# Splitting the second block of a seven-product matrix step, and giving the last tile the common order

## The chip, the cores and the metric

The kernel runs on one NeuronCore of a Trainium2 chip. The metric is the device time of one execution in microseconds (us). Before the change the median of three runs is 280.29 us (279.97 to 280.5). TensorE (PE) multiplies matrices and adds into PSUM banks, VectorE (DVE) and ScalarE (ACT) work element by element and empty PSUM, GpSimd (POOL) prepares some inputs and issues loads, SyncE (SP) issues the stores. Each engine runs its own instructions in order and waits for the others by semaphores.

## The reference

Two parts follow each other. The first is attention over pooled keys and values: for each of 8 batches and 8 heads, 576 queries of 64 elements meet 72 keys, each the mean of 8 neighbours.

```
scores = scale * q @ k_pooled.T          # 576 x 72 for each batch and head
attn   = exp(scores - max) ; attn /= sum(attn) + 1e-9
x      = attn @ v_pooled                  # 4608 tokens x 512 after joining the heads
h      = x @ w_in                         # 512 x 2048
g      = h * sigmoid(h)
out    = g @ w_out                        # 2048 x 512, float32
```

## The kernel before

The 4608 tokens are worked in nine tiles of 512, t = 0 to 8. Tile 0 uses plain products. Tiles 1 to 8 use `tile_products`, where both products of the second part are done as 2 x 2 block products with seven block multiplications in place of eight, plus additions of blocks. While tile t is multiplied, the attention of batch t + 1 is woven in between, so tiles 1 to 6 carry attention work and tiles 7 and 8 (called bare) carry none.

The order of the work in a tile is a written list of items. The first product is cut in four units a, b, c, d, and `a1` is block multiplication 1 of unit a, with four matmuls. `as`, `bs`, `cs`, `ds` only apply the activation to a finished block. For the second product, `P2` is the first half of block multiplication 2 and `Q2` its second half; `o2:4-5` is the part of it from contraction block 4 up to 5. Each of the eight contraction blocks of a multiplication is one **step** of two matmuls of 128x256 (L608, one for each half c of the tokens), so `P2` and `Q2` have four steps each. A step of a unit also has two matmuls. Tiles 2 to 6 follow `FOUR`, which ends in `HEAD`; tile 1 follows `THREE`, a text of its own; tiles 7 and 8 follow `BARE`, in which the second product is written out and `HEAD` isn't used. For tile 8 some text replacements are applied (L861). In a tile of `FOUR` the steps of the first product are 0 to 53 (and 62, 63 for `d4`); `P1` and `Q1` are 54 to 61, and the second product goes on from 64 to 111.

The second product uses three PSUM banks. Bank A takes multiplication 1, is copied to bank B by DVE (L618, in `behind`), and then takes multiplication 2 on top. Bank E takes multiplication 5; ACT copies it into SBUF as p (L621). B takes multiplication 6; then DVE forms E = B + p (L623). Then multiplication 7 goes on top of B, 3 on top of E, 4 on top of B. So the first step of `P7` writes the bank that L623 has just read, and must wait for it. When multiplication 2 ends, `second(2)` makes DVE copy A to the output tile (L653); the stores are issued after multiplication 3 (both 256-column halves together) and 4. In tile 8, B is split in two banks, one for each c, and L660 stands for L623, once for each half.

Multiplications 5, 6, 7, 3 take as their left operand sums of hidden blocks, `h_sum[0]` to `h_sum[3]`, formed by DVE (L537) in halves of four contraction blocks for sums 0, 1 and 2. `h_sum[0]` and `h_sum[1]` need the activations of `d4` and `ds`.

The banks come from two rings, `mm` of three and `at` of five. In tiles 2 to 6, a tile takes seven banks from `mm`, in this order: bank B of units a, b, c, d, then A, B, E of the second product. The attention takes its banks from `at`.

The attention, the sums and the loads are **fillers**: each has a step number s and is emitted just before step s + 1, wherever the list of items then is. In tiles 2 to 6 the sums stand at 64 to 66, at 77 the first denominators (den_ps L348, then ACT's lnd L357 and rec L358) and the second scores (sc_ps L330, then four exponentials es L338), at 87 the second denominators and two sets of numerators (nu_ps L374, then DVE's xT L383), and at 94 the third scores. Fillers keep their step number when the items are reordered.

Of the kernel before, what the change touches and what calls it, by code (L numbers as in the profile page):

```python
# [36 lines left out]
def kernel(  # L37
# [759 lines left out]
    def load_half_2(name, half):  # L797
        for i0, i1 in ((0, SA), (SA, SLOTS), (SLOTS, SLOTS + 1)):
            load_slots(nc.gpsimd, 2, name, i0, i1, half)

    HEAD = "P1 ds Q1 d4 P2 Q2 P5 Q5 P6 Q6 P7 Q7 P3 Q3 P4 Q4"
    FOUR = (
        "a1 a5 b1 b5 a6 a2 b6 b2 a7 a3 b7 b3 as a4 c1 c5 bs b4 d1 c6 c2 d5 d6 c7 c3 d2 d7"
        " cs d3 c4 " + HEAD
    )
# [9 lines left out]
    for t in range(NT):  # L815
# [42 lines left out]

        order = ORDER.get(t, FOUR if a < B else BARE)
        if t == NT - 1:  # L860
            order = order.replace("P4 Q4", "R4 S4").replace("o5:0-1 o2:0-3 o5:1-8", "o5:0-2 o2:0-2 o5:2-8").replace("o2:3", "o2:2")  # L861
        o = 2 if t == 1 else 0
        f = []

# [95 lines left out]
```

## Time and profile before

| what | value |
|---|---|
| time, median of three runs | 280.29 us |
| the profiled execution's own time | 280.23 us |
| its span, first to last instruction | 278.4 us |
| TensorE busy | 270.7 us (97%) |
| VectorE busy | 209.6 us (75%) |
| ScalarE busy | 190.6 us (68%) |
| GpSimd busy | 97.3 us (35%) |
| DMA, mean over the span | 135 GB/s |
| granted TensorE clock | full in all 40 slices |

In the profile PE is a matmul, PEld the load of its stationary operand, L608 a line of the kernel and o_psA, o_psB, o_psE the three banks of the second product. A line of the timeline gives the start, the length, the engine, the line and operation, what is written from what, and how many instructions are merged. Times count from the start of the span. The second product of tile 2 starts at 93.15 us, those of tiles 3 to 6 at 121.85, 150.55, 179.19 and 207.84, of tile 7 at 236.49 and of tile 8 at 261.08.

### The profile page before, as it was taken

What the parts mean: (1) busy time and instruction counts of PE and PEld (TensorE: products, weight loads), DVE (VectorE), ACT (ScalarE), POOL (GpSimd) and SP (SyncE); (2) the same over time, 40 slices, a digit from 0 to 9 for tenths busy, and PEclk for the clock granted to TensorE, in tenths of its full rate; (3) what the DMA queues carried; (4) which work ended last, traced back from release to release, by engine and by line L of the source; (5) the groups of instructions that cost most, each with busy time, mean ns of one, the idle gap of its engine ahead of it and who ended that gap; (6) DMA issues with size and microseconds to landing.
All of it is one profiled execution on the core that took longest, in us unless ns stands there. A gap on an engine that the chain in (4) does not pass through costs nothing.

```text
span 278.4 us, 7274 instructions
## 1 busy us (share of the span) xinstructions
PE 270.7 (97%) x2952; PEld 212.4 (76%) x2959; DVE 209.6 (75%) x388; ACT 190.6 (68%) x376; POOL 97.3 (35%) x102
## 2 busy tenths in 40 slices
PE   8999999999999999999999999999999999999994
PEld 4448544488788878887888778877887788888883
DVE  4787886987997867876787687777787686766872
ACT  1677766568669785979497958885798678409700
POOL 8665217232138520962087219850900000000000
PEclk9999999999999999999999999999999999999999
DMA  7999999897747896569556966998410032004004
GB/s 213 279 254 244 207 325 190 219 160 140 150 55 153 222 169 116 130 164 172 96 118 167 168 103 156 189 110 130 122 31 0 4 77 76 2 19 115 20 2 151
DMA packets 31473, 37.72 MB, mean 135 GB/s; under 512 B 10352, under 2 KB 22384, under 8 KB 31440
## 3 DMA queue, kind: packets, MB, share of 16 engines
q0 software_dynamic: 23792, 26.64, 52.4%
q1 hardware_dynamic: 7216, 9.97, 12.8%
q10 hardware_dynamic: 432, 0.66, 0.7%
q8 instruction: 23, 0.38, 0.6%
q14 instruction: 10, 0.08, 0.1%
HBM read 36.70 MB, written 9.44 MB: 166 GB/s over the span
## 4 chain that ended last, share of the span: by engine, by line
PE 87%; ACT 6%; DVE 4%; issue 1%; DVEq 0%
PE u_psB L589 14%; PE o_psB L608 13%; PE o_psA L608 10%; PE u_psA L589 10%; PE u_psE L589 10%; PE o_psE L608 9%; PE hp_ps L474 6%; PE o_ps L509 3%; PE sc_ps L330 3%; ACT es L338 3%; PE warm_ps L708 2%; PE den_ps L348 2%; DVE o_psE L623 2%; PE nu_ps L374 1%; DVE xT L383 1%; ACT rec L358 1%
## 5 line engine op out<-in xcount | busy, mean ns | idle before, releaser
L608 PEld LDWEIGHTS <-h_sum 128*128 128x128 bf16 x512 | 48.7, 98 | 10.1 <-issue 2.2
L589 PEld LDWEIGHTS <-w_sum 128*128 128x128 bf16 x496 | 48.2, 98 | 5.7
L338 ACT ACTIVATE es<-sc_ps 72x384 bf16<-72x384 f32 (+1 forms) x100 | 39.0, 469 | 13.9 <-PE sc_ps L330 13.8
L608 PEld LDWEIGHTS <-h_T 128*128 128x128 bf16 x384 | 36.5, 98 | 6.1 <-issue 1.1
L589 PEld LDWEIGHTS <-w_in_sb 128*128 128x128 bf16 x372 | 36.3, 98 | 4.4
L589 PE MATMUL u_psA<-xT,w_in_sb 128*128 128x256 bf16 x248 | 37.4, 273 | 0.0
L589 PE MATMUL u_psB<-x_sum,w_sum 128*128 128x256 bf16 x248 | 36.7, 273 | 0.0
L608 PE MATMUL o_psB<-w_sum,h_sum 128*128 128x256 bf16 x256 | 31.8, 273 | 1.4 <-DVE o_psE L623 1.4
L608 PE MATMUL o_psA<-w_out_sb,h_T 128*128 128x256 bf16 x256 | 31.0, 272 | 0.0
L618 DVE COPY u_psB<-u_psA 128x512 f32<-128x512 f32 x31 | 21.4, 697 | 10.5 <-PE u_psA L589 10.3
L623 DVE TENSOR_TENSOR u_psE<-u_psB,p 128x512 f32<-128x512 f32 x31 | 20.9, 693 | 9.7 <-ACT p L621 8.6
L627 ACT ACTIVATE h_T<-u_psE 128x512 bf16<-128x512 f32 x31 | 18.5, 597 | 11.2 <-PE u_psE L589 11.0
L383 DVE TENSOR_TENSOR xT<-nu_ps,rec 128x384 bf16<-128x384 f32 (+1 forms) x50 | 23.8, 530 | 0.2
L183 POOL TENSOR_TENSOR raw<-raw 72x1024 f32<-72x1024 f32 x10 | 23.6, 2362 | 0.0
L640 DVE TENSOR_TENSOR c<-u_psB,p 128x512 f32<-128x512 f32 x31 | 21.0, 680 | 3.1 <-PE u_psB L589 2.3
L537 DVE TENSOR_TENSOR h_sum<-h_T 128x1024 bf16<-128x1024 bf16 (+1 forms) x31 | 21.3, 698 | 1.1 <-ACT h_T L627 1.1
L627 ACT ACTIVATE h_T<-u_psB 128x512 bf16<-128x512 f32 x31 | 18.6, 600 | 4.4 <-PE u_psB L589 4.4
L537 DVE TENSOR_TENSOR h_sum<-h_T,h_sum 128x1024 bf16<-128x1024 bf16 (+1 forms) x24 | 20.4, 858 | 0.1
L627 ACT ACTIVATE h_T<-c 128x512 bf16<-128x512 f32 x31 | 19.7, 637 | 0.0
L627 ACT ACTIVATE h_T<-u_psA 128x512 bf16<-128x512 f32 x31 | 18.8, 607 | 1.2 <-PE u_psA L589 1.0
L357 ACT ACTIVATE lnd<-den_ps 128x384 f32<-128x384 f32 (+1 forms) x23 | 11.1, 484 | 11.9 <-PE den_ps L348 11.7
L474 PE MATMUL hp_ps<-xT,w_in_sb 128*128 128x288 bf16 (+2 forms) x122 | 18.8, 303 | 0.2
(87 smaller groups left out, 466.6 us busy)
## 6 DMA issues: line engine op xcount, KB each, us to landing
out_dram<-o_sb SPq DMA_DIRECT2D x128, 64.0 KB, 1.7
raw<-in_k_dram POOLq DMA_DIRECT2D x10, 576.0 KB, 8.6
raw<-in_v_dram POOLq DMA_DIRECT2D x10, 576.0 KB, 8.1
q_bf<-in_q_dram POOLq DMA_DIRECT2D x6, 576.0 KB, 9.1
w_in_sb<-in_moe_w_in_dram POOLq DMA_DIRECT2D x8, 256.0 KB, 8.4
w_out_sb<-in_moe_w_out_dram POOLq DMA_DIRECT2D x4, 512.0 KB, 13.3
raw<-in_v_dram POOLq DMA_DIRECT2D x2, 768.0 KB, 11.1
raw<-in_k_dram POOLq DMA_DIRECT2D x1, 768.0 KB, 9.5
```

Of the source, the lines that this page charges most:

```text
L183: nc.gpsimd.tensor_add(out=raw[:, :, : 2 * D], in0=raw[:, :, : 2 * D], in1=raw[:, :, 2 * D :])
L338: nc.scalar.activation(es[:, s, :], sc[s], func=AF.Exp, scale=score_scale)
L357: nc.scalar.activation(lnd, den_ps[:, :w], func=AF.Ln)
L383: nc.vector.tensor_mul(out=xT[:, 2 * g0 + c : 2 * (g0 + ng - 1) + c + 1 : 2, cols], in0=nu[c][:, :w].rearrange("r (g n) -> r g n", g=ng), ...
L474: nc.tensor.matmul(hp_ps[:, r0:r1], lhsT=w_in_sb[:, kk, g * 128 : (g + 1) * 128], rhs=xT[:, kk, x0 : x0 + r1 - r0], start=(kk == 0), stop= ...
L537: nc.vector.tensor_tensor(out=h_sum[n][:, k0:k1, :], in0=get(a), in1=get(b), op=op)
L589: nc.tensor.matmul(ps[y, BANK[n]][:, u, :], lhsT=w[:, kk, 128 * u : 128 * (u + 1)], rhs=x[:, kk, :], start=n in (1, 5) and u == 0 and kk == 0,
L608: nc.tensor.matmul(o_bank(n, c), lhsT=left(n, kt, c), rhs=w[:, kt, :], start=n in (1, 5) and kt == 0 and c == 0, stop=kt == KQ - 1, skip_g ...
L618: vcopy(out=ps[y, "B"], in_=ps[y, "A"])
L623: tt(out=ps[y, "E"], in0=ps[y, "B"], in1=f32[y], op=add)
L627: nc.scalar.activation(h_T[:, g : g + 2, j * NQ : (j + 1) * NQ], src, func=AF.Silu)
L640: tt(out=c22, in0=ps[y, "B"], in1=f32[y], op=add)
```

## The change

In tiles 2 to 6, multiplication 2 is cut after its fifth step. Its last three steps, and with them DVE's copy of bank A, now come after multiplication 6 and ahead of 7; multiplications 5 and 6 come three steps earlier. In tile 8 the two replacements that gave it an order of its own are gone, so that it has the order of tile 7 (save its last two items): one step of 5, three of 2, seven of 5, then 6, and the other five of 2. Tile 8 had two, two, six, and then the other six of 2. Nothing is added or left out; the number of matmuls, copies, sums and stores is the same.

```diff
-    HEAD = "P1 ds Q1 d4 P2 Q2 P5 Q5 P6 Q6 P7 Q7 P3 Q3 P4 Q4"
+    HEAD = "P1 ds Q1 d4 P2 o2:4-5 P5 Q5 P6 Q6 o2:5-8 P7 Q7 P3 Q3 P4 Q4"
...
         if t == NT - 1:
-            order = order.replace("P4 Q4", "R4 S4").replace("o5:0-1 o2:0-3 o5:1-8", "o5:0-2 o2:0-2 o5:2-8").replace("o2:3", "o2:2")
+            order = order.replace("P4 Q4", "R4 S4")
```

## The prediction

> **What bounds the kernel now.** I read the page first (busy shares, the chain that ended last), then the waits of PE, then the timeline of one tile of 2 to 6 and of the last tile, engine by engine.
>
> ```profile
> PE 270.7 (97%) x2952; PEld 212.4 (76%) x2959; DVE 209.6 (75%) x388; ACT 190.6 (68%) x376; POOL 97.3 (35%) x102
> ...
> PE 87%; ACT 6%; DVE 4%; issue 1%; DVEq 0%
> ```
>
> PE is the bound, and the chain leaves it for ACT and DVE in only a tenth of the span. So the change is worth what it takes from PE's holes. The waits of PE name two that it touches:
>
> ```profile
> PE o_psB L608 <- DVE o_psE L623: 1.4, 6, 0.3
> ...
> PE o_psE L608 <- DVE h_sum L537: 0.2, 1, 0.2
> ```
>
> The first stands six times, once in each of tiles 1 to 6, ahead of P7. The second is in the last tile. In tile 2 PE runs:
>
> ```profile
> 95.92 1.91 PE L608 MATMUL o_psA<-w_out_sb,h_T 128*128 128x256 bf16 x16
> 97.66 1.47 PE L608 MATMUL o_psE<-w_sum,h_sum 128*128 128x256 bf16 x12
> 99.07 0.37 PE L348 MATMUL den_ps<-es,ones 72*32 72x384 bf16 x4
> 99.37 0.54 PE L330 MATMUL sc_ps<-qT,kz 32*72 32x192 bf16 x16
> 99.84 0.61 PE L608 MATMUL o_psE<-w_sum,h_sum 128*128 128x256 bf16 x4
> 100.28 1.91 PE L608 MATMUL o_psB<-w_sum,h_sum 128*128 128x256 bf16 x16
> 102.12 0.34 PE L348 MATMUL den_ps<-es,ones 72*32 72x384 bf16 x4
> 102.30 0.83 PE L374 MATMUL nu_ps<-es,vp 72*32 72x192 bf16 x32
> 103.36 1.69 PE L608 MATMUL o_psB<-w_sum,h_sum 128*128 128x256 bf16 x14 [0.23 <-DVE o_psE L623]
> ```
>
> Sixteen matmuls take 97.66 - 95.92 = 1.74 us, so one takes 0.109 and a step 0.218. P7 could have started at 103.06, when its first weight load runs (in the same place P4 starts 0.43 after the start of 16 numerator matmuls; 16 more take 0.33, and 102.30 + 0.76 = 103.06). It started at 103.36, when L623 was through: 0.30 lost. ACT and DVE show why L623 was late:
>
> ```profile
> 99.54 0.49 ACT L357 ACTIVATE lnd<-den_ps 128x384 f32<-128x384 f32 x1 [0.48 <-PE den_ps L348]
> 100.06 0.52 ACT L358 ACTIVATE rec<-lnd 128x384 f32<-128x384 f32 x1
> 100.50 1.60 ACT L338 ACTIVATE es<-sc_ps 72x384 bf16<-72x384 f32 x4
> 101.98 0.59 ACT L621 COPY p<-o_psE 128x512 f32<-128x512 f32 x1
> ```
>
> ```profile
> 96.98 0.68 DVE L537 TENSOR_TENSOR h_sum<-h_T 128x1024 bf16<-128x1024 bf16 x1
> 97.58 0.68 DVE L537 TENSOR_TENSOR h_sum<-h_T,h_sum 128x1024 bf16<-128x1024 bf16 x1
> ...
> 102.60 0.70 DVE L623 TENSOR_TENSOR o_psE<-o_psB,p 128x512 f32<-128x512 f32 x1 [2.25 <-ACT p L621]
> 103.21 1.94 DVE L383 TENSOR_TENSOR xT<-nu_ps,rec 128x384 bf16<-128x384 f32 x4
> ```
>
> The copy p stands on ACT behind lnd, rec and four exponentials, because the fillers at step 77 come inside Q5. L623 then waits 2.25 us for p, and PE for L623. In the last tile the late one is the second half of h_sum[0]:
>
> ```profile
> 263.70 0.60 PE L608 MATMUL o_psE<-w_sum,h_sum 128*128 128x256 bf16 x4
> 264.14 0.60 PE L608 MATMUL o_psA<-w_out_sb,h_T 128*128 128x256 bf16 x4
> 264.58 0.60 PE L608 MATMUL o_psE<-w_sum,h_sum 128*128 128x256 bf16 x4
> 265.33 1.05 PE L608 MATMUL o_psE<-w_sum,h_sum 128*128 128x256 bf16 x8 [0.16 <-DVE h_sum L537]
> ```
>
> **Part 1, tiles 2 to 6.** Moved: six matmuls and their weight loads, and DVE's copy L653. No DMA moves: the store of that output tile is issued after Q3, far behind. The number of steps is the same, so the fillers stay where they are in time; den_ps and the scores now fall after the first step of P6 instead of inside Q5.
>
> *The wait at P7.* P5 starts at 95.92 + 5 x 0.218 = 97.01, P6 at 98.75. In tiles 7 and 8 p starts 0.25 after P6's first matmul (241.63 to 241.88; 266.22 to 266.47), so here at 99.00, ahead of lnd, and is done at 99.6 instead of 102.57. Multiplication 6 ends three steps ahead of 102.02, at 101.37; by tile 8's lag (Q6's end at 267.96, DVE's start at 268.12) to tile 7's (243.37, 243.64), L623 runs from about 101.6 to 102.3. P7 at 103.06 finds it done. Cover left: 0.7 us. Gain 0.30, and by the same reading 0.30, 0.29, 0.30 and 0.30 in tiles 3 to 6 (P7 at 132.06, 160.75, 189.40, 218.04 against 131.76, 160.46, 189.10, 217.74): 1.49 in all.
>
> The idle figures beside P7 are 0.22 or 0.23, 1.12 in sum for the five; I take starts against starts, since those are recorded. The Trainium skill, Perfetto Trace Analysis, section on the Tensor Engine instruction, says that a matmul's reported end is an estimate from its size and no observation. By the idle rows alone the whole change would come to 279.0 rather than 278.6.
>
> *p goes ahead of lnd, rec, es on ACT.* Behind it wait den_ps of step 87, and through it PE. ACT is idle 0.48 before lnd. Where nothing else holds the next instruction, ACT starts it 0.46 to 0.48 after p (256.64 to 257.10; 232.04 to 232.51), so lnd could start at 99.48, ahead of its 99.54: no cost. With the 0.62 of the p at 101.98 (there lnd waited for den_ps) it is 99.62: 0.08 later. The far end is p's whole 0.59, if it starts only when the idle time is over. The exponentials end at 102.10, and den_ps needs the last for its fourth matmul, so a delay reaches PE nearly in full. I take 0.01 a tile, 0.05 in all, near the unit rows since they show the same copy followed at once; ends 0 and 5 x 0.59 = 2.9.
>
> *P5 and Q5 come 0.65 earlier.* Their operands: the first half of h_sum[0] starts at 95.78 and is done at 96.46, needed at 97.01. The second half (the 96.98 row) is done at 97.66, needed at 97.88; after 0.06 from DVE's end to PE's start (265.27 to 265.33) 0.16 us is left. h_sum[1]'s second half, done at 98.26, is needed at about 99.8 to 100.4. Bank E's ring slot was unit d's, read by ACT from 95.53 to 96.13: 0.88 of slack. All zero; the thin one is Q5, 0.16. The other tiles have the same distances within 0.02.
>
> *L653 on DVE.* It goes behind L623, ends at about 102.95, and ahead of four xT. These now start at 102.9 instead of 103.21, if nu_ps is there (last numerators' start 102.9). Behind them PE's scores at step 94 wait for the third xT's bank: 102.9 + 3 x 0.485 = 104.35, needed at 104.67. Zero; were L653 0.3 later, its excess would count.
>
> *Bank A is held longer*, till 102.95 in place of 99.23. Its ring slot goes next to unit a of the next tile, filled by DVE's copy at 110.94: 8 us of slack, cost nothing. The Trainium skill, PSUM — Partial Sum Buffer, summary of rules, advises to evacuate promptly, which speaks against the change; it gives no price. If the 3.7 us of longer holding were a wait each time, the sum would be 18 us worse; the row's 8 us of slack say nothing of the kind happens.
>
> **Part 2, tile 8.** P5 to P6 is 263.70 to 266.22, 2.52 us for 20 matmuls that need 2.18: 0.34 lost. Tile 7 has the new order, and there it is 239.11 to 241.63, also 2.52, with 22 matmuls: 0.12 lost. So P6 stays put and one step more of multiplication 2 fits into the hole; five are left behind Q6 instead of six. P7 could start at 267.96 + 10 x 0.109 = 269.05 instead of 269.27. Its second matmul, at 269.16, needs L660's second half, which ends at 269.09, plus 0.06: 269.15. Just done. Its other edge: multiplication 2 starts at 263.92 in place of 264.14, and needs A's copies (L651, 263.03 to 263.80, plus 0.06): 0.06 left. Gain 0.22 at most, 0 at the lower end if both edges bind; I take 0.17.
>
> **Sum.** 1.49 - 0.05 + 0.17 = 1.6 from the profiled execution's 280.23: 278.6. That execution stands 0.06 below the median 280.29, so 278.7. Everything behind these points (xT, x_sum, POOL's gate, the next tile's first steps) is released by PE or follows it, with DVE and ACT idle before L670 and L672, so it moves along.
>
> **The rivals.**
>
> *Part of the gain goes into den_ps.* p delays lnd by 0.1 to 0.25, and PE waits at step 87 rather than at P7. For: only 0.06 of room on ACT. Against: the copies in the units. Five times 0.1 to 0.25 off: 279.2 to 279.9.
>
> *No gain.* Another release holds P7 at 103.36, or the scores at step 94 take the wait (bank release by xT). For: the step sits among attention fillers that wait on one another. Against: P7 has no wait other than L623's in the waits of PE. Then only tile 8 gains: 280.0 to 280.4.
>
> *Slower: Q5 waits for h_sum.* P5 and Q5 have come closer to sums that DVE makes in one run from 95.78 to 98.26. If the first step waits for the whole of h_sum[0], P5 stands from 97.01 to 97.72, 0.71 a tile; less the 0.30 gained, 0.41 x 5 - 0.17 = 1.9 worse: 282.1. Against: in tile 8 two steps of 5 run at 263.70, ahead of the second half's start at 264.58, so halves are tracked apart. It decides once the sums come 0.46 later than now (0.16 of room plus the 0.30 gained); one more DVE operation of 0.60 ahead of them would do.
>
> **How the numbers follow.** The forecast with its own range of 278.2 to 279.2 has 0.70; the partial gain 0.13; no gain 0.07; slower 0.10. A difference under 0.2%, 0.56 us, can't be told from none, so faster means below 279.73: 0.70 + 0.12 = 0.82; within, 0.01 + 0.07 = 0.08; slower 0.10. The range 278.2 (all of 1.49 + 0.34, and 0.3 for the spread of runs shown) to 279.9 holds the first two cases and leaves out 0.17 and a little of the first.
>
> **What would show it.** Right: the wait of P7 on L623 falls from six to one (tile 1), p starts right after P6's first matmuls, L623's wait for p is gone, P6 to P7 in tile 2 has no hole. Wrong: a wait of den_ps on es, of o_psE on h_sum, or of sc_ps on xT in each of tiles 2 to 6; or in tile 8, o_psB waiting on L660. The likeliest mistake is the 0.06 on ACT and the 0.16 at Q5, both taken from rows that end that close.

## The result, and the profile after

The median of six runs is 278.38 us (278.04 to 279.0) against 280.28 us of six runs of the kernel before (279.73 to 280.54). The ratio is 0.9935, 95% interval 0.992 to 0.9951, or 1.4 to 2.2 us. The forecast was 278.7, faster. One execution in a second timing of the changed kernel (below) took 456.98 us at a granted clock of 0.56, and is left out of that timing's median.

The page of the changed kernel, the busy shares and the chain that ended last:

```profile
PE 270.6 (98%) x2959; PEld 211.3 (77%) x2959; DVE 209.7 (76%) x388; ACT 190.7 (69%) x376; POOL 97.3 (35%) x102
...
PE 93%; DVE 4%; DMA 2%; issue 0%; DVEq 0%
```

ACT had 6% of the chain before and is no longer among the shares listed. The busy times of PE, DVE, ACT and POOL are within 0.1 us of those before; PE's 270.6 us now lie in a span of 276.3 us. The waits of PE, as the profile lists them:

```profile
PE warm_ps L708 <- DVE warm L727: 1.2, 1, 1.2
PE o_psB L608 <- DVE o_psE L623: 0.3, 1, 0.3
PE kz_ps L275 <- DVE k L257: 0.2, 1, 0.2
```

The wait of P7 on L623 is left once, in tile 1, whose order isn't changed; that of the last tile on h_sum is gone from the list. The timeline of tile 2 after the change, PE from P2 to P7:

```profile
95.33 1.25 PE L608 MATMUL o_psA<-w_out_sb,h_T 128*128 128x256 bf16 x10
96.41 1.91 PE L608 MATMUL o_psE<-w_sum,h_sum 128*128 128x256 bf16 x16
98.16 0.38 PE L608 MATMUL o_psB<-w_sum,h_sum 128*128 128x256 bf16 x2
98.47 0.37 PE L348 MATMUL den_ps<-es,ones 72*32 72x384 bf16 x4
98.77 0.54 PE L330 MATMUL sc_ps<-qT,kz 32*72 32x192 bf16 x16
99.24 1.70 PE L608 MATMUL o_psB<-w_sum,h_sum 128*128 128x256 bf16 x14
100.78 0.82 PE L608 MATMUL o_psA<-w_out_sb,h_T 128*128 128x256 bf16 x6
101.53 0.35 PE L348 MATMUL den_ps<-es,ones 72*32 72x384 bf16 x4
101.70 0.83 PE L374 MATMUL nu_ps<-es,vp 72*32 72x192 bf16 x32
102.47 1.70 PE L608 MATMUL o_psB<-w_sum,h_sum 128*128 128x256 bf16 x14
```

The same tile on ACT, and on DVE:

```profile
98.42 0.59 ACT L621 COPY p<-o_psE 128x512 f32<-128x512 f32 x1
98.95 0.49 ACT L357 ACTIVATE lnd<-den_ps 128x384 f32<-128x384 f32 x1
99.47 0.52 ACT L358 ACTIVATE rec<-lnd 128x384 f32<-128x384 f32 x1
99.90 1.60 ACT L338 ACTIVATE es<-sc_ps 72x384 bf16<-72x384 f32 x4
```

```profile
101.05 0.70 DVE L623 TENSOR_TENSOR o_psE<-o_psB,p 128x512 f32<-128x512 f32 x1 [1.89 <-PE o_psB L608]
101.66 0.68 DVE L653 COPY o_sb<-o_psA 128x512 f32<-128x512 f32 x1
102.26 1.94 DVE L383 TENSOR_TENSOR xT<-nu_ps,rec 128x384 bf16<-128x384 f32 x4
```

P7 starts 0.77 us after the numerators (1.06 before). The copy p now stands ahead of lnd, in a place where ACT was idle, and lnd still starts 0.48 after den_ps. L623 waits for PE's multiplication 6 and no longer for p. The last tile on PE, from its first step of multiplication 5 to P7:

```profile
261.73 0.38 PE L608 MATMUL o_psE<-w_sum,h_sum 128*128 128x256 bf16 x2
261.95 0.82 PE L608 MATMUL o_psA<-w_out_sb,h_T 128*128 128x256 bf16 x6
262.60 1.80 PE L608 MATMUL o_psE<-w_sum,h_sum 128*128 128x256 bf16 x14
264.24 1.91 PE L608 MATMUL o_psB<-w_sum,h_sum 128*128 128x256 bf16 x16
265.99 1.25 PE L608 MATMUL o_psA<-w_out_sb,h_T 128*128 128x256 bf16 x10
267.08 1.91 PE L608 MATMUL o_psB<-w_sum,h_sum 128*128 128x256 bf16 x16
```

P5 to P7 is 5.35 us, before 5.57 (263.70 to 269.27). P5 to P6 is 2.51 us, and 22 matmuls at 0.109 would take 2.40, so 0.11 of the wait at h_sum[0] is still there, too small to be listed.

Two lengths are used below, both from first matmul to first matmul: P2 to P4 in tile 2, and P2 of tile 2 to P4 of tile 8, which leaves out the front of the kernel. The second was 95.92 to 272.77 = 176.85 us before and is 95.33 to 270.57 = 175.24 after: 1.61 less. The two profiled executions differ by 280.23 - 278.04 = 2.19, and the other 0.59 lies ahead of P2 of tile 2, in code that the change doesn't touch.

### The profile page after: what moved, and what is told of

Same layout as the page of the kernel before. It is cut to its first block, busy times and chain, and to the rows that moved or that the text cites. A ratio compares the mean times of both kernels' runs of the same rounds, so it can differ in the third digit from the quotient of the medians.

```text
span 276.3 us, 7291 instructions
## 1 busy us (share of the span) xinstructions
PE 270.6 (98%) x2959; PEld 211.3 (77%) x2959; DVE 209.7 (76%) x388; ACT 190.7 (69%) x376; POOL 97.3 (35%) x102
## 4 chain that ended last, share of the span: by engine, by line
PE 93%; DVE 4%; DMA 2%; issue 0%; DVEq 0%
PE o_psB L608 16%; PE u_psB L589 15%; PE o_psA L608 10%; PE o_psE L608 10%; PE u_psA L589 10%; PE u_psE L589 10%; PE hp_ps L474 7%; PE sc_ps L330 4%; PE o_ps L509 4%; PE nu_ps L374 3%; PE den_ps L348 2%; DMA raw<-in_k_dram 2%; PE warm_ps L708 1%; DVE xT L383 1%; DVE w_sum L548 1%; DVE raw L253 1%
## 5 line engine op out<-in xcount | busy, mean ns | idle before, releaser
L608 PE MATMUL o_psB<-w_sum,h_sum 128*128 128x256 bf16 x256 | 32.7, 273 | 0.3 <-DVE o_psE L623 0.3
L608 PE MATMUL o_psA<-w_out_sb,h_T 128*128 128x256 bf16 x256 | 31.9, 272 | 0.0
L618 DVE COPY u_psB<-u_psA 128x512 f32<-128x512 f32 x31 | 21.4, 698 | 10.5 <-PE u_psA L589 10.3
L623 DVE TENSOR_TENSOR u_psE<-u_psB,p 128x512 f32<-128x512 f32 x31 | 20.9, 693 | 9.7 <-ACT p L621 8.6
```

What stands on the lines that cost most here:

```text
L608: nc.tensor.matmul(o_bank(n, c), lhsT=left(n, kt, c), rhs=w[:, kt, :], start=n in (1, 5) and kt == 0 and c == 0, stop=kt == KQ - 1, skip_g ...
L618: vcopy(out=ps[y, "B"], in_=ps[y, "A"])
L623: tt(out=ps[y, "E"], in0=ps[y, "B"], in1=f32[y], op=add)
```

## The experiments

All lengths from the profiles. "Whole" is P2 of tile 2 to P4 of tile 8.

| kernel | time, us (median) | whole, us | less than before | P2 to P4 of tile 2 |
|---|---|---|---|---|
| before | 280.2 to 280.4 | 176.85 | | 12.20 |
| changed | 278.38 | 175.24 | 1.61 | 11.92 |
| changed, timed again | 278.42 | 175.27 | 1.58 | 11.92 |
| tiles 2 to 6 alone | 278.89 | 175.47 | 1.38 | 11.92 |
| tile 8 alone | 279.99 | 176.63 | 0.22 | 12.20 |
| p late | 281.60 | 178.26 | -1.41 | 12.52 |
| no step behind Q6 | 278.35 | 175.25 | 1.60 | 11.92 |
| p late, L653 behind xT | 279.85 | 176.66 | 0.19 | 12.20 |
| one step behind Q6 | 281.25, one run | 178.27 | -1.42 | 12.53 |
| two steps | 279.25, one run | 176.13 | 0.72 | 12.09 |
| four steps | 279.45, one run | 175.58 | 1.27 | 11.98 |
| six steps | 281.64, one run | 177.76 | -0.91 | 12.42 |
| changed, more edits | 278.95 | 175.04 | 1.81 | 11.93 |
| changed, d4 first | 278.15 | 175.03 | 1.82 | 11.92 |

**The two parts apart.** Only the new `HEAD`, and only the removed replacements of L861.

> Only the new HEAD, tiles 2 to 6; tile 8 keeps its old order. Theory (each of the five tiles loses its wait of 0.28 us at P7, and nothing else changes): 1.40 us below the kernel before, 278.9 us; from the first matmul of P2 to that of P4, 11.92 us in tiles 2 to 6 (12.20 before); tile 8 as before, 0.34 us lost between P5 and P6. Rival (part of the 1.9 us between the medians comes from elsewhere in these tiles): more than 1.7 below.

> Only tile 8 takes the order of tile 7. Theory: 0.22 us less from P5 to P7 of tile 8, 280.05 us, hardly to be told from the kernel before by its time; in the profile P5 to P7 is 5.35 us instead of 5.57. Up to tile 7 the instructions are those of before, so the time at which P2 of tile 2 starts (95.92 before, 95.33 after the change) also shows how much the front moves from one run to the next. Rival (the front's 0.6 us comes with the change): 95.9 here.

The first is 278.89 us (ratio 0.9956, 0.9939 to 0.9973), the second 279.99 (0.9993, 0.9983 to 1.0002). In the profiles they take 1.38 and 0.22, together 1.60, against 1.61 for both at once. The front started P2 of tile 2 at 95.52 and at 96.11, early with the new `HEAD` and late without, as the rival would have it; later profiles speak against it, without excluding it (at the end of this section).

**Theory A, the place of p, against theory B, the steps as cover.** Before the change, p is late on ACT and no step stands between Q6 and P7. The change alters both. Two kernels have one each. The first issues p after multiplication 6:

```diff
-            elif n == 5:
+            elif n == 5 and not (y == "o" and 2 <= t <= 6):
                 f32[y] = f32_tile("p5", 3)
                 acopy(f32[y], ps[y, "E"])
             elif n == 6:
+                if y == "o" and 2 <= t <= 6:
+                    f32[y] = f32_tile("p5", 3)
+                    acopy(f32[y], ps[y, "E"])
                 tt(out=ps[y, "E"], in0=ps[y, "B"], in1=f32[y], op=add)
```

> The changed kernel, but in tiles 2 to 6 ACT's copy p of bank E is issued after multiplication 6, so behind the second exponentials, as before the change; the three steps between Q6 and P7 stay. Theory A (the place of p on ACT is what made L623 late): p starts with the end of the exponentials, L623 0.5 us later, and P7 waits 0.28 us again in each of the five tiles: 1.4 us above the changed kernel, 279.8. Theory B (the three steps between Q6 and P7 are what covers L623): no loss, 278.4.

The second leaves p early and puts the three steps ahead of P6:

```diff
-    ... P2 o2:4-5 P5 Q5 P6 Q6 o2:5-8 P7 Q7 ...
+    ... P2 o2:4-5 P5 Q5 o2:5-8 P6 Q6 P7 Q7 ...
```

> The changed kernel, but in tiles 2 to 6 the last three steps of multiplication 2 stand ahead of P6, so no step lies between Q6 and P7; p keeps its early place on ACT. Theory A (the place of p): L623 runs from 0.26 us after Q6's end, for 0.70, and the second denominators and numerators take 1.04, so P7 waits under 0.05 a tile: 278.4 to 278.6. Theory B (the three steps as cover): the wait of 0.28 a tile is back, 279.8.

Without the cover the kernel is as fast as the changed one: 278.35 us (ratio 0.9942, 0.9925 to 0.996). Its PE, ACT and DVE in tile 2, the lines around Q6 and P7 (each fence one engine):

```profile
100.01 1.91 PE L608 MATMUL o_psB<-w_sum,h_sum 128*128 128x256 bf16 x16
101.85 0.35 PE L348 MATMUL den_ps<-es,ones 72*32 72x384 bf16 x4
102.03 0.83 PE L374 MATMUL nu_ps<-es,vp 72*32 72x192 bf16 x32
102.79 1.70 PE L608 MATMUL o_psB<-w_sum,h_sum 128*128 128x256 bf16 x14
```

```profile
98.74 0.58 ACT L621 COPY p<-o_psE 128x512 f32<-128x512 f32 x1
```

```profile
102.03 0.70 DVE L623 TENSOR_TENSOR o_psE<-o_psB,p 128x512 f32<-128x512 f32 x1 [1.13 <-PE o_psB L608]
```

From P2 to P6 PE takes 4.36 us here as before the change (95.65 to 100.01; 95.92 to 100.28), so p's place is what differs. L623 ends at 102.73 and P7 starts at 102.79, 0.76 after the numerators: no wait, but nothing to spare either, since 0.06 is also what lay between L623's end and P7 when P7 waited (103.30 to 103.36). With p late, the wait is back in all five tiles although three steps stand behind Q6, and more is lost than expected: 281.60 us (ratio 1.0053, 1.0036 to 1.007), slower than the kernel before. Its PE, ACT and DVE in tile 2:

```profile
101.99 0.84 PE L374 MATMUL nu_ps<-es,vp 72*32 72x192 bf16 x32
103.05 1.69 PE L608 MATMUL o_psB<-w_sum,h_sum 128*128 128x256 bf16 x14 [0.22 <-DVE o_psE L626]
104.67 0.86 PE L330 MATMUL sc_ps<-qT,kz 32*72 32x192 bf16 x16
```

```profile
101.67 0.59 ACT L625 COPY p<-o_psE 128x512 f32<-128x512 f32 x1
```

```profile
102.30 0.70 DVE L626 TENSOR_TENSOR o_psE<-o_psB,p 128x512 f32<-128x512 f32 x1 [2.84 <-ACT p L625]
102.90 0.68 DVE L656 COPY o_sb<-o_psA 128x512 f32<-128x512 f32 x1
103.50 1.94 DVE L383 TENSOR_TENSOR xT<-nu_ps,rec 128x384 bf16<-128x384 f32 x4
```

(L623, L653 and L621 of the other kernels are L626, L656 and L625 here.) Theory A is shown and B falls. But theory A priced only P7. The third scores (sc_ps) take 0.86 us instead of 0.54: the copy of bank A now stands on DVE behind the late L623 and ahead of xT, which empties the numerators' banks and so makes room for the scores, whose banks come from the same ring. If so, moving that copy behind xT takes the second loss away:

```diff
-            elif n == 2:
+            elif n == 2 and not 2 <= t <= 6:
                 vcopy(out=o_sb[0][:, :, LO], in_=ps["o", "A"])
...
             elif n == 7:
+                if 2 <= t <= 6:
+                    vcopy(out=o_sb[0][:, :, LO], in_=ps["o", "A"])
```

> As the kernel with the late p, and DVE's copy L653 of tiles 2 to 6 is moved behind the numerators' xT (ahead of L670). In the late p's profile the third scores took 0.86 us instead of 0.54. If that is because L653, standing behind the late L623, held back xT and so the scores' banks, the 0.32 goes and the wait at P7 alone is left: 12.20 us from P2 to P4 (12.51 with the late p), 280.0 us. If the scores wait for something else, 12.5 and 281.6.

It does: 279.85 us (ratio 0.9985, 0.9972 to 0.9999), 12.20 us from P2 to P4, and scores of

```profile
104.86 0.54 PE L330 MATMUL sc_ps<-qT,kz 32*72 32x192 bf16 x16
```

So the cut of multiplication 2 has a price of its own, 0.32 us a tile, that falls due when L623 is late and the copy stands ahead of xT.

**How many steps behind Q6.** The order of the changed kernel with another cut: `P2 o2:4-7 ... o2:7-8` for one step, `P2 o2:4-6 ... o2:6-8` for two, `P2 ... Q2` for four, `o2:0-2 ... o2:2-8` for six; five wasn't tried. Each was run once, beside a run of the kernel before that took 279.79 us, so the lengths from the profiles are what counts here.

> The changed kernel, but in tiles 2 to 6 only one step of multiplication 2 stands behind Q6 (seven ahead of P5). Then multiplication 5 ends after the fillers of step 77 and p is issued behind the second exponentials, as before. Theory A (place of p): all of the gain in these tiles is lost; and since L653 now follows the late L623 ahead of xT, the third scores wait for a bank as they did with the late p: 12.5 us from P2 to P4 (12.20 before, 11.92 after the change). Theory B (what counts is the number of steps behind Q6): a step less of wait for every step moved, so 0.2 us gained, 12.0.

> The changed kernel with two steps of multiplication 2 behind Q6. Multiplication 5 ends just ahead of the fillers of step 77, so p is still issued ahead of lnd, but its data come 0.22 us later: lnd, rec and the second exponentials are 0.15 to 0.22 later and the second den_ps waits for the last of them up to 0.1. Theory A: 11.92 to 12.05 us from P2 to P4 in tiles 2 to 6. Theory B: 11.92 as well, or 0.1 more.

> The changed kernel with four steps behind Q6. Q5 needs the second half of h_sum[0]; in the profile after the change that is done 1.74 us after P2's start, plus 0.06, and Q5's first matmul now falls 1.74 after it: a wait of 0.06 a tile, 11.98 us from P2 to P4. If the room at Q5 is larger than I read it, 11.92.

> The changed kernel with six steps behind Q6. P5's first matmul falls 0.44 us after P2's start and waits for the first half of h_sum[0] till 0.59 (0.15); Q5 then waits for the second half till 1.80 (0.34 more): 0.49 a tile, 12.41 us from P2 to P4, 2.4 us above the changed kernel. If the halves were waited for together at P5, the wait would stand whole at P5's first matmul: 1.36 a tile there, of which the eight matmuls of P5 then no longer run under it, 13.3.

One step is worse than none (12.53), as theory A has it: ACT's line for p in its tile 2 shows it back behind the exponentials.

```profile
101.59 0.59 ACT L621 COPY p<-o_psE 128x512 f32<-128x512 f32 x1
```

With two steps p comes ahead of lnd, but so late that lnd slips, and the second den_ps waits for the exponentials and the numerators come behind it: 12.09, which is 0.17 over the changed kernel where at most 0.13 was expected. The exponentials end 6.35 us after P2 (101.99), in the changed kernel 6.17 (101.50). From ACT and PE:

```profile
98.95 0.59 ACT L621 COPY p<-o_psE 128x512 f32<-128x512 f32 x1 [0.17 <-PE o_psE L608]
99.43 0.50 ACT L357 ACTIVATE lnd<-den_ps 128x384 f32<-128x384 f32 x1
...
100.39 1.60 ACT L338 ACTIVATE es<-sc_ps 72x384 bf16<-72x384 f32 x4
```

```profile
101.84 0.52 PE L348 MATMUL den_ps<-es,ones 72*32 72x384 bf16 x4
102.05 0.98 PE L374 MATMUL nu_ps<-es,vp 72*32 72x192 bf16 x32
```

lnd starts 0.64 after its den_ps (98.79), against 0.48 with three steps. Four steps give 11.98 and six 12.42, as worked out from the times of h_sum[0]; with six the wait stands in PE's own line:

```profile
98.24 1.05 PE L608 MATMUL o_psE<-w_sum,h_sum 128*128 128x256 bf16 x8 [0.16 <-DVE h_sum L537]
```

Three is the best of the cuts tried: with fewer, p is late; with more, the sums are.

**Beyond the change.** Two waits were left: tile 1's at P7, and 0.12 us at h_sum[0] in each of tiles 7 and 8.

```diff
-        "c4 P1 ds Q1 d3 d4 o5:0-1 ..."
+        "c4 P1 ds Q1 d4 d3 o5:0-1 ..."
...
-        " ds d4 P2 Q2 P5 Q5 P6 Q6 P7 Q7 P3 Q3 P4 Q4"
+        " ds d4 P2 o2:4-7 P5 Q5 P6 Q6 o2:7-8 P7 Q7 P3 Q3 P4 Q4"
...
-            for n, (sc, den) in enumerate(zip((63, 77, 94), (77, 87, 103))):
+            x = 78 if t == 1 else 77
+            for n, (sc, den) in enumerate(zip((63, x, 94), (x, 87, 103))):
```

> The changed kernel and two more edits where its profile still shows PE waiting. Tile 1: one step of multiplication 2 behind Q6 and the fillers of step 77 one step later, so that p goes ahead of lnd there too: its wait of 0.33 us at P7 goes. Tiles 7 and 8: d4 ahead of d3, so that the activation which h_sum[0] needs comes 0.44 us sooner: the 0.12 us that each loses at the fifth step of multiplication 5 goes. Together 0.57 below the changed kernel, 277.8 us, if nothing new waits; in tile 1 the room at Q5 is only 0.06 by the profile, and if that is gone 0.1 of it is lost.

278.95 us (ratio 0.9946, 0.9927 to 0.9965), no gain over the changed kernel. Tiles 7 and 8 did gain 0.12 each. Tile 1, which lies ahead of the length called whole, lost: P2 to P4 is 12.56 us there (67.37 to 79.93) and is 12.25 in the changed kernel (66.63 to 78.88). P5 stands 0.2 us waiting for the first half of h_sum[0], and P3 meets a new wait, since L653 now delays xT and h_sum[3] behind it:

```profile
77.47 1.92 PE L608 MATMUL o_psE<-w_out_sb,h_sum 128*128 128x256 bf16 x16 [0.17 <-DVE h_sum L537]
```

The first edit alone:

> The changed kernel with the second of the two edits alone: in tiles 7 and 8 d4 goes ahead of d3. By the profile that had both edits, P5 to P6 is 2.40 us there instead of 2.52, so 0.24 in all and nothing lost elsewhere: 278.2 to 278.4 us, by its time not to be told from the changed kernel, by its profile 0.12 us less from P5 to P6 in each of the two tiles.

278.15 us (ratio 0.9927, 0.9911 to 0.9943); P5 to P6 in tiles 7 and 8 is 2.40 us, and the whole is 175.03, 0.21 to 0.24 under the two profiles of the changed kernel. By its time alone it can't be told from that kernel.

**The changed kernel again.**

> The changed kernel once more, beside the kernel before on the same chip. The profiles give 5 x 0.28 + 0.22 = 1.62 us, the first timing 1.9. If the rest was spread between runs, 1.6 here, 278.6 us, and the front (P2 of tile 2) anywhere from 95.3 to 96.4, where the profiles so far have it; if the change does more than the profiles show, 1.9 again.

278.42 us, the median of five runs (ratio 0.9934, 0.9916 to 0.9952), and 175.27 in its profile. The kernel before took 280.34 beside it, so the medians are 1.9 apart again, which by the expectation speaks for a change that does more than the profiles show. P2 of tile 2 starts at 95.61. It lay from 95.33 to 96.44 in the profiles of the kernels whose code is the same up to there: at 95.92 and 96.11 with the old order of tiles 2 to 6, from 95.33 to 95.81 with the new one, from 95.53 to 96.44 with the other cuts. So the front moves by up to 1.1 us from one execution to the next, and the 0.59 between the two profiles needs no other cause, though two profiles of the old order don't exclude one. Why the medians lie 1.9 apart, and the profiles behind the front 1.6, isn't settled; 1.6 is inside both intervals. The medians less the whole are 103.4 to 103.5 for the kernel before, 103.1 for the changed one, 103.4 for each of its two parts alone, and 103.3 for the kernel with p late, which has both parts. So, as far as medians of 5 to 17 runs tell, the 0.3 that is over follows neither part.

## Why the prediction was right

*The wait at P7* (said: 1.49 for five tiles). Right in mechanism and cause; measured 0.28 a tile from P2 to P4, and 1.38 in the whole with the new `HEAD` alone. P2 to P7 did shrink by 0.30 (7.44 to 7.14), but P7 to P4 grew by 0.02 (4.76 to 4.78). Taking starts against starts was the better reading: the five idle figures beside P7, which begin at the reported end of the numerators (102.30 + 0.83 = 103.13 in tile 2), sum to 1.12 only. The Trainium skill, Perfetto Trace Analysis, section on the Tensor Engine instruction, calls such an end an estimate; this case agrees with it in that more was gained than the idle time shown.

*The cause.* The prediction named both p's place on ACT and the steps left as cover, and gave 0.7 us of cover. The runs show that the place alone does it; the three steps behind Q6 could stand ahead of P6, and what they add is room: L623 ends 0.72 us ahead of P7 with them (101.75 to 102.47), 0.06 without. What the cut is for is to let multiplication 5 end ahead of the fillers of step 77.

*p ahead of lnd* (said: 0.05, room 0.06). Cost nothing that PE shows: lnd starts 0.48 after den_ps, 0.47 before, and the second den_ps 6.20 after P2 in both (95.92 to 102.12; 95.33 to 101.53). That the room is about that small is shown by the two-step cut, where 0.22 more cost 0.17.

*Q5 and h_sum* (said: 0.16 of room). Shown by the four-step cut: one step more, 0.22, cost 0.06. The rival on the other side, that P5 waits for both halves at once, has against it the six-step cut, where two separate waits came out at 0.50 as worked out.

*L653 on DVE* (said: zero; 0.3 later and its excess would count). Zero in the changed kernel; 0.32 a tile with p late, and gone once the copy stood behind xT.

*Bank A held longer* (said: zero). No profile lists a wait on it; the copy that next takes its place, L618, waits only for PE's u_psA in the lists.

*Tile 8* (said: 0.17, at most 0.22). 0.22; neither edge of 0.06 and less bound. The reading from tile 7, that P6 stays put, holds to 0.01: P5 to P6 is 2.51 (2.52 before).

*The sum* (said: 1.49 - 0.05 + 0.17 = 1.61) is 1.61 in the profiles. That it agrees so closely is partly luck: the term for P7 was 0.11 too large, and the charge on ACT (0.05) and the term for tile 8 (0.05 too small) happen to make up for it. The rest of the 1.9 between the medians was in no term of the sum, and whether it belongs to the change stays open.

## What to carry to other kernels

When an engine waits for a short operation, look at what that operation stands behind on its own in-order queue; letting it be issued ahead of work that is inserted there can be worth more than putting work in front of the waiter. A moved block takes its own copy-out along, and that copy has a new place on another queue: price it there as well. Where the front of a kernel varies, compare lengths between two instructions behind it instead of whole times.

## What the runs showed of the hardware that was not expected

The time at which the front of the kernel is through varies by up to 1.1 us between executions (P2 of tile 2 at 95.33 to 96.44), while from there on two profiles of the same order agree to within 0.03 us over 175 (175.24 and 175.27). At least the late ones go with late loads: DVE's second group of v sums (L253), which waits for its load in all the profiles, starts at 13.66 and 13.68 us where P2 is at 96.43 and 96.44, and at 12.53 where it is at 95.33; among the earlier ones the two don't keep step (12.42 with 95.81). One step of 0.22 us decided whether a tile took 12.53, 12.09 or 11.92 us (one, two, three steps behind Q6): the price isn't proportional to the work moved. From three to two, where p keeps its place on ACT but comes later, it is 0.17; from two to one, where p falls behind the exponentials, 0.44.
